# Moving the loads of a streaming attention decode from SyncE's queue to GpSimd's, with a one-packet flag

## The chip, the core and the metric

The kernel runs on one core of a Trainium2 chip. The metric is the device time of one execution in microseconds (us). Before the change it is 1918.17 us in the median of three runs (1917.4 to 1920.89).

## The reference

One token attends to a cache of 32 heads, 32,768 keys and values each, 192 wide, in bf16; a small dense block follows. Cut to what matters:

```python
q = (layernorm(x) @ wq).reshape(1, 1, 32, 192)              # 640 -> 6144
scores = einsum("bhqd,bhkd->bhqk", q, k_cache) * 192 ** -0.5
o = einsum("bhqk,bhkd->bhqd", softmax(scores), v_cache)
h = x + o.reshape(1, 1, 6144) @ wo
out = h + relu(layernorm(h) @ w1) @ w2
```

Both caches together are 805 MB, read once. Every other input is small beside them.

## The kernel before

A head's keys come in two loads of 6 MB into kt0 and kt1. Its values come in two loads of 3 MB into vb, one after the other, and one of 6 MB into va. In each, a partition receives one contiguous row of 48 KB or 24 KB. SyncE issues every load, when the buffer's last readers are done:

```python
def dma_program(g):                      # runs on SyncE
    def load(dst, src, sem, *label):
        g.do(lambda: nc.sync.dma_start(out=dst, in_=src), sem, label, by=16)
    ...
    for c in range(DT):                  # 5 loads of wq
        load(wq_c[c], ..., f"dwq{c}", "wq", c)
    for h in range(LAST):
        keys(h, 0); vals(h, 0); keys(h, 1)
        for ld in ((2, 1) if h == 0 else (1, 2)):
            vals(h, ld)                  # vals(h, 1) first waits for ("PV", h, 1)
        if h % 2 == 0:
            ...                          # wo of two heads
```

The loads of head 0 are thus keys 0, values 0 (vb), keys 1, values 2 (va), values 1 (vb again). GpSimd waits for each landing and passes it on with a semaphore increment, which TensorE (PE) and VectorE (DVE) wait for. PE takes a head's chunks in a fixed order; the first values are needed at its third chunk. ScalarE (ACT) copies and exponentiates.

The softmax here doesn't subtract the row's maximum and nothing guards it: scores larger than these inputs give would overflow.

## Time and profile before

| | before |
|---|---|
| time, median | 1918.17 us |
| span of the profiled run | 1915.3 us |
| busiest compute engine | DVE, 82% |
| DMA engines | full in all slices but the last, 431 GB/s |
| queue | one, SyncE's, 29,616 packet records |

The prediction below shows and reads the lines. In short: the stream of rows sets the pace of this kernel until the last keys land (at 1864.51 us; the DMA share is 1.00 from 120 to 1850 us); some 50 us of compute follow.

### The profile page before, as it was taken

What the parts mean: (1) busy time and instruction counts of PE and PEld (TensorE: products, weight loads), DVE (VectorE), ACT (ScalarE), POOL (GpSimd) and SP (SyncE); (2) the same over time, 40 slices, a digit from 0 to 9 for tenths busy, and PEclk for the clock granted to TensorE, in tenths of its full rate; (3) what the DMA queues carried; (4) which work ended last, traced back from release to release, by engine and by line L of the source; (5) the groups of instructions that cost most, each with busy time, mean ns of one, the idle gap of its engine ahead of it and who ended that gap; (6) DMA issues with size and microseconds to landing.
All of it is one profiled execution on the core that took longest, in us unless ns stands there. A gap on an engine that the chain in (4) does not pass through costs nothing.

```text
span 1915.3 us, 36109 instructions
## 1 busy us (share of the span) xinstructions
PE 1551.1 (81%) x15899; PEld 1085.0 (57%) x15899; DVE 1561.3 (82%) x731; ACT 939.5 (49%) x2000; POOL 1.0 (0%) x6
## 2 busy tenths in 40 slices
PE   7778887887878788877878877778788787877888
PEld 7555555655555555555556555556555555555555
DVE  2797787987878978789787888878798787987897
ACT  2455454554544544545545445445355454554444
POOL 0000000000000000000000000000000000000000
PEclk9888998888988889888898888898888898888988
DMA  9999999999999999999999999999999999999998
GB/s 409 430 434 433 430 435 431 435 436 433 434 431 434 435 429 431 435 432 439 434 429 435 434 431 435 434 429 437 431 434 438 431 436 429 437 431 433 431 432 367
DMA packets 29650, 825.29 MB, mean 431 GB/s; under 512 B 3131, under 2 KB 4668, under 8 KB 8124
## 3 DMA queue, kind: packets, MB, share of 16 engines
q1 hardware_dynamic: 29616, 824.98, 99.9%
q8 instruction: 15, 0.25, 0.0%
q14 instruction: 7, 0.06, 0.0%
q10 hardware_dynamic: 12, 0.00, 0.0%
HBM read 824.97 MB, written 0.00 MB: 431 GB/s over the span
## 4 chain that ended last, share of the span: by engine, by line
DVE 39%; DMA 38%; PE 15%; ACT 6%; issue 1%; DVEq 0%; POOLq 0%; SPq 0%
DMA kt<-in_A_k_cache_dram 36%; DVE sc L706 19%; DVE pr L703 18%; PE o_ps L360 7%; PE tp L379 6%; ACT kT L606 5%; DMA va<-in_A_v_cache_dram 2%; PE sp L360 1%; DVE o_pair L718 1%; ACT pA L621 1%; DVE oT L728 0%; DMA kt<-in_A_wq_dram 0%; DVE rec L711 0%; DVE rec L712 0%; DVE odd L724 0%
## 5 line engine op out<-in xcount | busy, mean ns | idle before, releaser
L703 DVE TENSOR_TENSOR pr<-kt,qb 128x2304 f32<-128x2304 bf16 (+2 forms) x257 | 756.7, 2944 | 314.8 <-POOLq L321 286.7
L606 ACT COPY kT<-tp 128x1024 bf16<-128x1024 bf16 (+1 forms) x898 | 814.3, 1017 | 272.9 <-PE tp L379 272.9
L379 PE MATMUL tp<-ident_f,kt 128*128 128x128 f32 x3456 | 588.4, 331 | 239.5 <-POOLq L342 162.9
L706 DVE TENSOR_REDUCE sc<-pr 128x12 f32<-128x2304 f32 (+2 forms) x257 | 756.1, 2942 | 8.9
L379 PEld LDWEIGHTS tp<-ident_f,kt 128*128 128x128 f32 x3456 | 482.7, 170 | 291.2 <-POOLq L342 168.7
L360 PE MATMUL o_ps<-va,pB 128*2 128x384 bf16 x1152 | 222.1, 341 | 65.0 <-POOLq L342 65.0
L360 PEld LDWEIGHTS sp<-qm,kT 128*128 128x128 bf16 x6912 | 197.2, 98 | 83.9 <-issue 42.8
L360 PE MATMUL sp<-qm,kT 128*128 128x2 bf16 x6912 | 214.5, 164 | 25.9 <-ACT pB L612 24.4
L360 PE MATMUL o_ps<-vb,pB 128*2 128x384 bf16 x1152 | 213.1, 331 | 22.9 <-ACT pA L621 22.3
L621 ACT ACTIVATE pA<-sc 128x12 bf16<-128x12 f32 (+2 forms) x257 | 58.2, 226 | 346.1 <-DVEq L65 346.1
L612 ACT ACTIVATE pB<-sp 128x20 bf16<-128x20 f32 (+2 forms) x258 | 52.4, 203 | 310.3 <-PE sp L360 310.3
L360 PEld LDWEIGHTS o_ps<-va,pB 128*2 128x2 bf16 x1152 | 94.4, 86 | 161.5 <-POOLq L342 72.4
L360 PE MATMUL o_ps<-va,pA 128*2 128x384 bf16 x896 | 172.2, 334 | 0.0
L360 PE MATMUL o_ps<-vb,pA 128*2 128x384 bf16 x896 | 166.7, 326 | 0.0
L360 PEld LDWEIGHTS o_ps<-vb,pB 128*2 128x2 bf16 x1152 | 89.9, 84 | 122.2 <-ACT pA L621 28.2
L360 PEld LDWEIGHTS o_ps<-va,pA 128*2 128x2 bf16 x896 | 77.4, 86 | 76.1 <-issue 9.6
L360 PEld LDWEIGHTS o_ps<-vb,pA 128*2 128x2 bf16 x896 | 75.2, 84 | 70.2
L612 ACT ACTIVATION_READ_ACCUMULATOR pB<-sp 128x1 f32 x258 | 55.1, 214 | 0.0
L621 ACT ACTIVATION_READ_ACCUMULATOR pA<-sc 128x1 f32 x257 | 53.1, 206 | 0.0
L360 PE MATMUL o_ps<-xn_ln,kt 128*96 128x1 bf16 (+1 forms) x316 | 22.3, 208 | 2.7 <-DMA kt<-in_A_wq_dram 2.7
L360 PEld LDWEIGHTS o_ps<-xn_ln,kt 128*96 128x96 bf16 (+1 forms) x316 | 22.1, 174 | 2.8 <-issue 2.7
L718 DVE TENSOR_SCALAR o_pair<-o_ps,rec 2x384 bf16<-2x384 f32 x32 | 19.4, 605 | 1.5 <-PE o_ps L360 0.4
(69 smaller groups left out, 186.5 us busy)
## 6 DMA issues: line engine op xcount, KB each, us to landing
kt<-in_A_k_cache_dram SPq DMA_DIRECT2D x62, 6144.0 KB, 26.8
vb<-in_A_v_cache_dram SPq DMA_DIRECT2D x63, 3072.0 KB, 20.8
va<-in_A_v_cache_dram SPq DMA_DIRECT2D x31, 6144.0 KB, 26.8
kt<-in_A_k_cache_dram SPq DMA_DIRECT2D x3, 3072.0 KB, 21.3
wo_s<-in_A_wo_dram SPq DMA_DIRECT2D x16, 480.0 KB, 19.0
kt<-in_A_wq_dram SPq DMA_DIRECT2D x4, 1536.0 KB, 10.9
va<-in_A_v_cache_dram SPq DMA_DIRECT2D x1, 3072.0 KB, 30.7
va<-in_A_v_cache_dram SPq DMA_DIRECT2D x2, 1536.0 KB, 35.5
```

Source lines behind the costliest of these rows:

```text
L360: return lambda: pe.matmul(o, lhsT=w, rhs=r, **kw)
L379: calls.append(lambda b=b, o=o: pe.transpose(out=dst[:, b, :], in_=src[:, o:o + 2 * P].bitcast(f32), identity=ident_f[:]))
L606: g.do(lambda: act.copy(out=kT[c % 2][:, b0:b0 + nb, :], in_=src[:, 0:nb, :].bitcast(bf16)), "act_pe", ("cp", h, c, k))
L612: g.do(lambda: act.activation(out=pB[c % NB][:, 0:jp], in_=sp[:, 0:jp], func=F.Exp, scale=SCALE, accum_out=dsums[:, 2 * c + 1:2 * c + 2]), ...
L621: g.do(lambda: act.activation(out=pA[c % NB][:, 0:jd], in_=sc[c % NC][:, 0:jd], func=F.Exp, scale=SCALE, accum_out=dsums[:, 2 * c:2 * c + ...
L703: g.chain(lambda: dve.tensor_tensor(out=pr[:, 0:j1 - j0, :], in0=src[:, (off + j0) * Dh:(off + j1) * Dh].rearrange("p (j d) -> p j d", d=D ...
L706: g.chain(lambda: dve.reduce_sum(out=sc[c % NC][:, j0:j1], in_=pr[:, 0:j1 - j0, :], axis=X), "dve")
L718: g.do(lambda: dve.tensor_scalar_mul(out=o_pair[:, :, 1, :], in0=o_ps[0:2, 0:2 * Dh].rearrange("q (i d) -> q i d", i=2), scalar1=rec[0:2, ...
```

## The change

Its intent is to take the cost of a packet out of the stream. The call that issues a load from GpSimd is given a flag, `single_packet`, that I took to ask for one packet for each load and DMA engine. Seven first loads stay on SyncE, because nothing has to be waited for there; SyncE passes on the landings in GpSimd's place. The place in the order of loads where the issuing goes over from SyncE to GpSimd is called the seam below.

```diff
-    def dma_program(g):
+    def first_loads(g):
         def load(dst, src, sem, *label):
             g.do(lambda: nc.sync.dma_start(out=dst, in_=src), sem, label, by=16)
+        for c in range(DT):
+            load(wq_c[c], ..., f"dwq{c}", "wq", c)
+        load(kt[0][:], rows(k_hd, 0, 0, JK), "dk_first", "k", 0, 0)
+        load(vb[:], rows(v_hd, 0, 0, JK)[:, 0:JL * Dh], "dv_first", "v", 0, 0)
+
+    def dma_program(g):
+        e = nc.gpsimd
+        ... (the two set-up instructions that GpSimd had before)
+        def load(dst, src, sem, *label):
+            g.do(lambda: e.dma_start(out=dst, in_=src, single_packet=True), sem, label, by=16)
...
-        g.do(lambda: nc.gpsimd.sem_inc(sems["pool_pe"], 1))
+        g.do(lambda: nc.sync.sem_inc(sems["pool_pe"], 1))
...
         @block.sync
-            dma_program(Program(book, sems, nc.sync))
+            relay_program(Program(book, sems, nc.sync))
         @block.gpsimd
-            pool_program(Program(book, sems, nc.gpsimd))
+            dma_program(Program(book, sems, nc.gpsimd))
```

More of the change, by code (lines that the diff above doesn't have):

```diff
@@ L221 @@
     names = ["pool_pe", "act_pe", "dve_pe", "act_dve", "dve_act", "dve", "dve_row", "pe_dve", "pool_row", "pool_dve", "pool_act", "pe_act", "pe", "dve_sp", "act_row"]
-    names += [f"dk{i}" for i in range(NK)] + ["dva", "dvb"] + ["dwo", "dx", "dout"] + [f"dwq{i}" for i in range(5)]
+    names += [f"dk{i}" for i in range(NK)] + ["dva", "dvb", "dk_first", "dv_first"] + ["dwo", "dx", "dout"] + [f"dwq{i}" for i in range(5)]
     names += [f"dke{i}" for i in range(4)] + ["dvh0", "dvh1"] + [f"dve{i}" for i in range(4)] + ["dw1"] + [f"dw2_{i}" for i in range(4)]
@@ L227, with rows @@
              "dve": ("pool_dve", "act_dve", "pe_dve", "dve")}
-    def dma_program(g):
+    def rows(src, h, k0, jl):
+        return src[h, k0:k0 + P * jl, :].rearrange("(p j) d -> p (j d)", p=P)
+    def first_loads(g):
         def load(dst, src, sem, *label):
             g.do(lambda: nc.sync.dma_start(out=dst, in_=src), sem, label, by=16)
-        def rows(src, h, k0, jl):
-            return src[h, k0:k0 + P * jl, :].rearrange("(p j) d -> p (j d)", p=P)
+        for c in range(DT):
+            load(wq_c[c], wq_view[:, c * H * Dh:(c + 1) * H * Dh], f"dwq{c}", "wq", c)
+        load(kt[0][:], rows(k_hd, 0, 0, JK), "dk_first", "k", 0, 0)
+        load(vb[:], rows(v_hd, 0, 0, JK)[:, 0:JL * Dh], "dv_first", "v", 0, 0)
+    def dma_program(g):
+        e = nc.gpsimd
+        g.do(lambda: e.memset(wide[:], 0.0), "pool_act", ("ident0",))
+        g.wait("ident0")
+        g.do(lambda: e.affine_select(out=wide[:], in_=wide[:], compare_op=A.not_equal, fill=1.0, base=HE,
+                                     pattern=[[-1, HE + P + 2 * (P - HE)]], channel_multiplier=1), "pool_row", ("ident",))
+        def load(dst, src, sem, *label):
+            g.do(lambda: e.dma_start(out=dst, in_=src, single_packet=True), sem, label, by=16)
         def keys(h, ld):
@@ L257, in vals @@
             load((vb, vb, va)[ld][:], src, "dva" if ld == 2 else "dvb", "v", h, ld)
-        for c in range(DT):
-            load(wq_c[c], wq_view[:, c * H * Dh:(c + 1) * H * Dh], f"dwq{c}", "wq", c)
         for h in range(LAST):
-            keys(h, 0)
-            vals(h, 0)
+            if h > 0:
+                keys(h, 0)
+                vals(h, 0)
             keys(h, 1)
@@ L310, in dma_program, with relay_program @@
             load(w2_s[:, c0:c1], B_w2.rearrange("(c p) n -> p c n", p=P)[:, c0:c1], f"dw2_{i}", "w2", i)
-    def pool_program(g):
-        e = nc.gpsimd
-        g.do(lambda: e.memset(wide[:], 0.0), "pool_act", ("ident0",))
-        g.wait("ident0")
-        g.do(lambda: e.affine_select(out=wide[:], in_=wide[:], compare_op=A.not_equal, fill=1.0, base=HE,
-                                     pattern=[[-1, HE + P + 2 * (P - HE)]], channel_multiplier=1), "pool_row", ("ident",))
+    def relay_program(g):
+        first_loads(g)
         def key(h, ld):
             relay(g, "k", h, ld)
-            g.do(lambda: nc.gpsimd.sem_inc(sems["pool_dve"], 1))
+            g.do(lambda: nc.sync.sem_inc(sems["pool_dve"], 1))
             book_relay(g, "k", h, ld, sem="pool_dve")
@@ L797 @@
     plan = Program(book, sems)
-    for f in (dma_program, pool_program):
+    for f in (relay_program, dma_program):
         f(plan)
```

## The prediction

> **What bounds the kernel now.** I read the page first: busy shares, then the DMA row of the slices and the packet count.
>
> ```profile
> PE 1551.1 (81%) x15899; PEld 1085.0 (57%) x15899; DVE 1561.3 (82%) x731; ACT 939.5 (49%) x2000; POOL 1.0 (0%) x6
> ...
> DMA  9999999999999999999999999999999999999998
> ...
> DMA packets 29650, 825.29 MB, mean 431 GB/s; under 512 B 3131, under 2 KB 4668, under 8 KB 8124
> ...
> q1 hardware_dynamic: 29616, 824.98, 99.9%
> ```
>
> No compute engine is above 82%, while the DMA row is full in every slice but the last, and one queue (q1, SyncE's) keeps the 16 DMA engines occupied for 99.9% of the span. The kernel streams both caches once; its time is the transfer plus a start and a tail. The table of stretches says where the rest is (columns: length, busy time of the engines, clock, DMA share, GB/s).
>
> ```profile
> 120.00:1850.00 1730.00, 1402.17 (x14250) 975.43 (x14249) 1438.17 (x647) 861.19 (x1832) 0.00 (x0) 0.88 1.00 433
> 1850.00:1916.00 66.00, 56.61 (x645) 37.13 (x642) 51.42 (x38) 31.42 (x72) 0.00 (x0) 0.90 0.91 382
> ```
>
> In the long middle the DMA share is 1.00 at 433 GB/s. The chain that ended last shows the tail: the last head's keys, then compute alone.
>
> ```profile
> 1836.82 27.69 DMA kt<-in_A_k_cache_dram
> 1864.56 0.04 issue
> 1864.61 1.86 PE tp L379 x15
> ```
>
> So up to about 1864 us a microsecond taken from the stream is a microsecond of the span, and each microsecond in which the queue is empty is lost; the last 50 us are PE and ACT work that this change does not touch.
>
> The packet records of the same trace (start, length, bytes of each) give the grain. The median packet of 49,152 B takes 1815 ns, of 24,576 B 912, of 12,288 B 460, of 3,840 B 149, of 1,280 B 55, and a 4 B semaphore write 9. A straight line through them is bytes / 27.2 B per ns plus 8 ns. Per engine q1 has 29,616 / 16 = 1,851 packets: 825 MB / 16 / 27.2 gives 1,896 us of bytes, 1,851 x 8 ns gives 15 us of packet cost, and the sum is the 1,912.5 us that the records add up to. This 15 us is the only thing in the stream that the change can take.
>
> [...] The trace shows a constant cost per packet too, but of 8 ns; on 48 KB rows it is 0.44%, small but paid 1,851 times. [...] Here SyncE issued at 0.96 us and the first data packet began at 1.97 us; GpSimd's is not in this trace.
>
> **The change, part by part.**
>
> *Packets, minus.* Seven loads stay with SyncE (five of wq, the first keys, the first values): 5 x 9 + 9 + 9 = 63 packets per engine with their semaphore writes. The other 188 loads carry 1,851 - 63 = 1,788. With one packet for each load and engine, 188 are left if the semaphore write rides in the same packet, 376 if not: 1,412 to 1,600 packets fewer, times 8 ns, 11.3 to 12.8 us. About 130 of them (vectors and weights of the tail) lie behind the last keys, where compute is the limit, so 1 us is not earned. **Gain 11 us**, if the cost belongs to the packet and not to the descriptor: no run shows that yet, I give it 70%.
>
> *Issue latency, little.* What the queue still has to do when a load is issued is its slack. I replayed all issues with the packet lengths above, each load behind the one before. Past the first head the smallest slack is 2.6 us for a load into vb and 3.2 for one into kt; medians are 7.0 and 9.7. [...] If it took over 2.5 us, perhaps a third of the 31 heads would lose a fraction each. **Plus 0 to 3, I take 0.5.**
>
> *Relay, nothing.* The pass-on of a landing moves from GpSimd to SyncE: 17 ns in the trace, the same wait and increment on another sequencer. GpSimd had 1.0 us of work in all. DVE, PE and ACT keep their order of instructions.
>
> *Start, the risk.* Here are two queues at once. The change keeps GpSimd's first load (second half of head 0's keys) behind the end of the queries, as before:
>
> ```profile
> 33.03 0.33 SPq L232 DMA_DIRECT2D kt<-in_A_k_cache_dram  x1
> 33.40 0.43 SPq L232 DMA_DIRECT2D va<-in_A_v_cache_dram  x1
> 37.65 5.54 PEld L379 LDWEIGHTS tp<-ident_f,kt 128*128 128x128 f32 x27 [3.83 <-POOLq L342]
> 47.03 1.78 PE L360 MATMUL o_ps<-vb,pB 128*2 128x384 bf16 x10 [1.18 <-ACT pA L621]
> 54.57 0.33 SPq L232 DMA_DIRECT2D vb<-in_A_v_cache_dram  x1
> ```
>
> At 33 us SyncE's queue still holds the last rows of the first keys (passed on at 37.6) and all eight rows per engine of the first values (their packets end at 44.6). In one queue the new loads stand behind them. [...] The bytes are the same, but the first values then land after both, at 37 + 29 + 7 = 73 us instead of 45[...]. The tensor engine needs the values at its third chunk; the release of vb, seen at 54.57, is about 10 us behind them. So vb would be asked for at 82 to 84 us with nothing queued since 73: 10 to 13 us of empty queue, plus some 3.5 before the next head's first keys. **Plus 13 to 17 us if whole packets alternate; 0 if the engines mix finer or the old queue wins.**
>
> *Tail, little.* w1 and w2 are 40 + 96 rows per engine[...]. I take 0.
>
> **The sum.** Good case: 1918.2 - 11 + 0.5 = 1907.5. Alternating case: 1907.5 + 15 = 1922. The arithmetic leaves me between two lumps. [...]that keeping seven loads on SyncE looks like the work of someone who watched the start favours the first. I choose near the middle, a little to the good side: **1911 us**.
>
> **The rivals.**
> (a) *Alternating packets starve the start*: as above, 1918 to 1926. [...] Against it: only the first two loads can overtake anything; after 75 us there is one data queue.
> (b) *The 8 ns belong to the descriptor*: then nothing is gained and the time is 1918 to 1921 without, up to 1935 with the start's loss. For it: the 4 B semaphore write costs the same 8 ns although it follows its rows directly.
> (c) *GpSimd is slow at writing descriptors*, and its issue takes the place of the queue as the bound[...]. A microsecond over it in every head costs 31 us: 1938. Against it: most loads have 7 us and more. I give it 6%.
> (d) *Instruction fetches wait behind long packets*: the trace has them as 16 KB packets on a queue of their own, one each 11 to 18 us in the first 153 us and again from 1867 on. [...]
>
> **Range and chances.** The good case, up to 5 us better if semaphore writes ride along and start or tail gain: 1902 and up. The bad one with (d) ends at 1928. The range 1902 to 1928 holds both lumps. Faster by 2% would be 1880 us, under the 1,896 us that the bytes alone take, so it is all but excluded (1%); over 1956 needs (c) in full (3%).
>
> **What would show it.** Packet cost: the count of packets falls from 29,650 to some 4,000 or 7,000, if the records are of packets, or the rows' own records shorten from 1815 to 1807 ns; the middle stretch rises from 433 to 435 GB/s at the same 1.00 share. If it stays at 433, the gain is refuted. Start: the first pass-on of keys later than 37.6 us, the first use of vb later than 47, and a DMA share under 1.00 between 70 and 100 us refute the good case. Issue latency: a share under 1.00 in the middle. Tail: the stretch from the last keys' landing to the end should stay at 50 us.

The sum came to 1918.2 - 11 + 0.5 = 1907.5 us in the good case and to 1907.5 + 15 = 1922 in the other, and 1911 was chosen between them. The 0.5 was a guess. The 15 are an estimate on a condition that no trace showed, "if whole packets alternate": the 29 us in it are two loads of eight rows of 1815 ns for an engine, the 7 the eight rows of 912 ns of the first values. Rival (d)'s term, an estimate of up to 5 us on top of the other case, is in the 1928. In rival (c), "over it" is over the slack of 2.6 us. The 435 GB/s are 16 times the fitted 27.2 B per ns.

## The result

The changed kernel takes 1920.24 us in the median of four runs (1919.19 to 1922.07), beside 1919.53 of the kernel before (four runs, 1917.4 to 1921.38). The ratio is 1.0005, with a 95% interval of 0.9991 to 1.0020. The predicted gain of 7 us isn't there; the time is the same.

The profile page of the changed kernel:

```profile
PE 1551.9 (81%) x15899; PEld 1083.6 (56%) x15899; DVE 1561.4 (81%) x731; ACT 938.8 (49%) x2000; POOL 101.5 (5%) x194
...
DMA packets 27026, 825.29 MB, mean 430 GB/s; under 512 B 3131, under 2 KB 3132, under 8 KB 5500
...
q0 software_dynamic: 25984, 807.68, 97.5%
q1 hardware_dynamic: 1008, 17.30, 2.1%
```

GpSimd (POOL) is now busy for 101.5 us and not for 1.0, nearly all of it in the instructions that issue its loads, about 0.53 us each, beside everything else. The bytes moved to its queue, q0. But the packets number 27,026, not the 4,000 to 7,000 of the prediction. By stretches (columns as in the prediction), first the start of the kernel before, then the changed kernel:

```profile
40.00:80.00 40.00, 29.42 (x312) 21.64 (x311) 38.63 (x15) 25.22 (x50) 0.00 (x0) 0.87 1.00 429
80.00:120.00 40.00, 33.05 (x348) 21.25 (x347) 28.28 (x16) 18.25 (x41) 0.00 (x0) 0.98 1.00 427
```

```profile
40.00:80.00 40.00, 24.82 (x266) 16.59 (x265) 38.63 (x15) 22.67 (x43) 1.06 (x2) 0.79 0.98 417
80.00:120.00 40.00, 35.09 (x389) 22.49 (x387) 24.95 (x15) 20.59 (x48) 2.63 (x5) 0.99 0.98 411
120.00:1850.00 1730.00, 1403.14 (x14250) 976.10 (x14251) 1440.87 (x648) 859.98 (x1828) 86.12 (x163) 0.88 1.00 433
```

The middle runs at 433 GB/s and a share of 1.00, to the digit as before. That refutes the gain by the prediction's own test. What was lost lies before 120 us, where the DMA share is 0.98 for 80 us and was 1.00. The packet records show more. The median record, read from the traces:

```
bytes    before, SyncE's queue     changed, GpSimd's queue
49,152   1815 ns  x11904           1815 ns  x11776
24,576    912 ns  x8576             912 ns  x8448
 7,680    291 ns  x256              291 ns  x1280   (mostly two 3,840 B rows joined)
 3,840    149 ns  x2048             none
```

A long row is a record of its own, of the same length as before. Short rows alone are joined. From the same records one can read when a share of all bytes has arrived. Such marks compare streams better than spans do, and I use them below:

| | 4% | 6% | 30% | 90% | 98% |
|---|---|---|---|---|---|
| before, us | 79.75 | 118.65 | 576.56 | 1718.77 | 1870.59 |
| changed, us | 80.92 | 121.78 | 579.64 | 1721.36 | 1873.40 |
| behind, us | 1.2 | 3.1 | 3.1 | 2.6 | 2.8 |

So 3.1 us are lost by 120 us, and half a microsecond comes back in the middle. How far such marks scatter shows the run without the flag, further below: its records turn out to be the same, and its marks lie 0.7 to 1.2 us before the changed kernel's, with 2.4 us lost at 6%. Differences of a microsecond between two marks are not read here. The timeline of the start shows what happened (start, length, engine, line, operation, tiles; in brackets the idle time before and what ended it):

```profile
33.25 0.68 POOL L250 DMA_DIRECT2D kt<-in_A_k_cache_dram  x1 [31.30 <-PE attT L371]
...
37.63 4.71 PE L390 MATMUL tp<-ident_f,kt 128*128 128x128 f32 x27 [3.79 <-SPq L353]
...
59.35 3.36 PE L371 MATMUL o_ps<-vb,pB 128*2 128x384 bf16 x10 [13.67 <-SPq L353]
...
69.65 0.53 POOL L250 DMA_DIRECT2D vb<-in_A_v_cache_dram  x1 [35.19 <-PE o_ps L371]
...
81.73 0.53 POOL L250 DMA_DIRECT2D kt<-in_A_k_cache_dram  x1 [11.02 <-PE o_ps L371]
```

The first keys are used at 37.63 as before, so nothing overtook them. The first values are used at 59.35 and not at 47.03: PE stood 13.67 us for them; the same line before had 1.18. The next load of vb was issued at 69.65 instead of 54.57, the next head's keys at 81.73 instead of 78.37. The engines had run, or were running, out of rows by then: by the records they miss 0.4 us in all around 72 us and 1.3 around 82, and the first rows after a gap take up to 3159 ns in place of 1815.

The chain that ended last shows a second, smaller loss in the changed kernel's tail:

```profile
1841.38 25.39 DMA kt<-in_A_k_cache_dram
...
1866.85 3.42 PE tp L390 x15
```

The same 15 transposes took 1.86 us before. Now PE had waited 1.81 us for these keys, and the table of stretches gives the granted clock (the last three columns are clock, DMA share and GB/s), first for before, then for the changed kernel:

```profile
1864.00:1868.00 4.00, 3.86 (x49) 2.96 (x46) 3.82 (x3) 3.26 (x7) 0.00 (x0) 1.00 0.97 416
```

```profile
1867.00:1870.50 3.50, 3.50 (x22) 3.19 (x23) 3.44 (x2) 2.78 (x5) 0.00 (x0) 0.56 1.00 426
```

After the wait PE runs at a clock of 0.56 where it had 1.00. The traces of later runs show the same at these 15 transposes. Two of them, without the flag and with nine loads from SyncE:

```profile
1865.64 3.28 PE L390 MATMUL tp<-ident_f,kt 128*128 128x128 f32 x15 [1.81 <-SPq L353]
```

```profile
1872.59 3.33 PE L394 MATMUL tp<-ident_f,kt 128*128 128x128 f32 x15 [1.79 <-SPq L357]
```

In four traces PE waits 1.79 to 2.05 us here, a drop of the clock begins within half a microsecond of the first transpose and lasts 3.4 us, and the transposes take 3.28 to 3.44 us (this kernel, these two runs, and 8 KB pieces without the flag). In five it waits under 0.4 us, the clock over them is full, and they take 1.84 to 1.86 (before, 8 KB pieces with the flag and from SyncE, the run that waits for the landing, eleven loads from SyncE). So the drop goes with the wait at this place. That the wait causes it is not shown, and it is no rule: elsewhere in the trace of before only 15 of 66 idle times of 1.8 us or more have a drop begin within half a microsecond of their end.

The last keys land 2.3 us later than before (1866.77, not 1864.51), the transposes end 3.8 us later, the span 4.1 us. So of the 4.1 us between the two profiled spans 2.3 come with the stream and 1.8 arise in the tail. They are one execution each, the one of before among the fastest of its four and that of the changed kernel among the slower; the timed runs bound the difference at -1.7 to 3.8 us, and with 0 in that interval no loss of time is shown.

### The profile page after: what moved, and what is told of

Same layout as the page of the kernel before. It is cut to its first block, busy times and chain, and to the rows that moved or that the text cites. A ratio compares the mean times of both kernels' runs of the same rounds, so it can differ in the third digit from the quotient of the medians.

```text
span 1919.4 us, 36109 instructions
## 1 busy us (share of the span) xinstructions
PE 1551.9 (81%) x15899; PEld 1083.6 (56%) x15899; DVE 1561.4 (81%) x731; ACT 938.8 (49%) x2000; POOL 101.5 (5%) x194
## 2 busy tenths in 40 slices
DMA packets 27026, 825.29 MB, mean 430 GB/s; under 512 B 3131, under 2 KB 3132, under 8 KB 5500
## 4 chain that ended last, share of the span: by engine, by line
DVE 39%; DMA 37%; PE 14%; ACT 6%; issue 2%; another core or an unknown queue 1%; DVEq 0%; SPq 0%; POOL 0%
DMA kt<-in_A_k_cache_dram 37%; DVE sc L717 19%; DVE pr L714 18%; PE o_ps L371 6%; PE tp L390 6%; ACT kT L617 6%; PE sp L371 1%; DVE o_pair L729 1%; ACT pA L632 1%; DVE oT L739 0%; DVE rec L722 0%; DVE rec L723 0%; DVE odd L735 0%; DVE o_pair L741 0%
## 5 line engine op out<-in xcount | busy, mean ns | idle before, releaser
L250 POOL DMA_DIRECT2D kt<-in_A_k_cache_dram x67 | 35.6, 531 | 840.5 <-PE o_ps L371 809.2
L250 POOL DMA_DIRECT2D vb<-in_A_v_cache_dram x66 | 34.9, 529 | 806.0 <-PE o_ps L371 806.0
L623 ACT ACTIVATION_READ_ACCUMULATOR pB<-sp 128x1 f32 x258 | 55.4, 215 | 0.0
## 6 DMA issues: line engine op xcount, KB each, us to landing
vb<-in_A_v_cache_dram SPq DMA_DIRECT2D x1, 3072.0 KB, 55.4
```

The source lines that it names most:

```text
L250: g.do(lambda: e.dma_start(out=dst, in_=src, single_packet=True), sem, label, by=16)
L623: g.do(lambda: act.activation(out=pB[c % NB][:, 0:jp], in_=sp[:, 0:jp], func=F.Exp, scale=SCALE, accum_out=dsums[:, 2 * c + 1:2 * c + 2]), ...
```

## The experiments

My theory after the result: the flag changes nothing, a long row is the unit of both cost and alternation, and what the changed kernel loses it loses where two queues are in flight. The rivals: the flag works, but cost or alternation lie elsewhere; GpSimd's later start of a load is the loss; GpSimd's queue is slower or faster by itself. Marks are from one profiled execution of each; times have three rounds, or five where said.

### No flag

```diff
-    e.dma_start(out=dst, in_=src, single_packet=True)
+    e.dma_start(out=dst, in_=src)
```

> The changed kernel with the one-packet flag taken away and nothing else. Theory: the 8 ns belong to each row that an engine moves, and the flag changes nothing that can be measured here. Then the time is the changed kernel's, ratio to before 1.000 to 1.003, a 49,152 B row still takes 1815 ns, the record count stays at 27,026 (the short wo rows still joined in pairs of 7,680 B), and the first values still land near 57 to 59 us. Rival: the flag does frame a load as one packet, and part of the cost or of the start's alternation comes from it. Then rows get longer than 1815 ns or short rows are no longer joined (29,650 records), or the first values land at another time than 59 us.

Measured: 1919.34 us beside 1917.73, ratio 1.0005 (0.9989 to 1.0022). The page of this run:

```profile
DMA packets 27026, 825.29 MB, mean 430 GB/s; under 512 B 3131, under 2 KB 3132, under 8 KB 5500
```

Every record size and count is the changed kernel's, and the median lengths too: 1815 ns for the long rows, the short ones joined as with the flag. The first values land 55.2 us after their issue, with the flag 55.4. The flag did nothing that shows. GpSimd's queue joins the short rows here without it, too (27,026 records, not 29,650). Why the flag is without effect, no run tells.

### Pieces of 8 KB: what costs, and what an engine finishes before it switches

```diff
-    e.dma_start(out=dst, in_=src, single_packet=True)
+    e.dma_start(out=dst, in_=src, single_packet=True, max_dma_last_dim=8192)   # with the flag
+    e.dma_start(out=dst, in_=src, max_dma_last_dim=8192)                       # without
```

> The changed kernel with every row of GpSimd's loads cut into pieces of at most 8,192 B (six for a 48 KB row), flag kept: up to 49 pieces for a load and engine. Theory (cost for each piece, whatever the flag): 4,760 more pieces per engine at 8 ns are 38 us, ratio to before 1.018 to 1.022, and a piece takes 309 ns. Rival (cost for each packet, which the flag makes one for a load and engine): no longer than the changed kernel, ratio 0.998 to 1.004. At the start the order of pieces in the two queues shows what an engine finishes before it switches: one piece of 8 KB for one row of SyncE's (first values then land near 48 us) or six (59 us) or a whole load (59 us and later).

> As the run before it, with the flag taken away. Theory: the flag is without effect, so everything is as with it: ratio to before 1.018 to 1.022, piece 309 ns, same record count and the same order at the start. Rival (the flag makes one packet): this run is 38 us longer than the run with the flag, and engines switch between the queues more often at the start.

Measured: with the flag 1941.87 us, ratio 1.0117 (1.0100 to 1.0134); without it 1941.94, ratio 1.0121 (1.0104 to 1.0138). With the flag, and then without:

```profile
DMA packets 103186, 825.29 MB, mean 425 GB/s; under 512 B 3131, under 2 KB 3132, under 8 KB 6268
```

```profile
DMA packets 103186, 825.29 MB, mean 425 GB/s; under 512 B 3131, under 2 KB 3132, under 8 KB 6268
```

The two are alike again. Pieces do cost, so the rival of a free ride in one packet falls. But the size was missed: 22 us beside the changed kernel's 1920.24, and not the 38 of the theory. The records add up to more than the time in which they lie: a piece's record is 309 ns, of which some 3 overlap the next (an estimate: the 8 ns by the lengths less the 4.8 below). The marks give the true cost: from 30% to 90% of the bytes the stream takes 1155.9 us in both, against 1142.2 before; 13.7 us over 0.6 x 4,760 pieces is **4.8 ns** for each. (Counting the records between the marks, against the changed kernel or before, gives 4.7 to 4.8.)

The order at the start shows the alternation. The records carry no engine number; I strung them into 16 chains, each record behind one that ends where it begins. One chain from 31 us on (s is SyncE's queue, G GpSimd's, with KB; the last rows of the first keys are s48, the first values s24):

```
changed kernel   s48 s48 s48 s24 s24 G48 s24 G48 s24 G48 s24 G48 s24 G48 s24 G48 s24 G48 G48 G48
8 KB pieces      s48 s48 s48 s24 s24 s24 G8 s24 G8 s24 G8 s24 G8 s24 G8 s24 G8 G8 G8 G8 ...
```

In these chains an engine takes one row, or piece, from each queue in turn. With 8 KB pieces little can overtake a row of SyncE's, and the first values land 43.3 us after their issue in place of 55.4. With a 48 KB row between any two of them they are 12 us later. Alternation is real, but by rows, with the flag set.

These two runs also test what the loss at the start comes from, better than the runs that I made for it: issuer and seam are the changed kernel's, and only the rows of GpSimd's queue are shorter. The values are used at 47.22 and 47.42 us, and the 6% marks are at 120.6 and 120.9. The kernel before with the same pieces, next below, is at 120.2. So some 0.5 us are lost to it, or 1 if that kernel's 96 further pieces are set off (at 4.7 ns, an estimate), where whole rows lost 2.4 to 3.1. Most of the loss goes when the rows between the values get short; the rest is near the scatter of the marks.

### Pieces of 8 KB from SyncE

```diff
-    nc.sync.dma_start(out=dst, in_=src)          # the kernel before
+    nc.sync.dma_start(out=dst, in_=src, max_dma_last_dim=8192)
```

> The kernel before, SyncE issuing everything, with every row cut into pieces of at most 8,192 B: 4,856 more pieces per engine. Theory: a piece costs the same whoever issues it. From the two runs with GpSimd's pieces, whose bytes from 30% to 90% took 1155.9 us against 1142.2 in the kernel before, a piece costs 4.8 ns (the records overlap by some 3 ns, so their 8 ns are too much): 23 us, ratio to before 1.010 to 1.014. Rival: GpSimd's queue already joins the cost of several pieces and SyncE's does not. Then this one pays the 8 ns of its records, 39 us, ratio 1.018 to 1.022.

Measured: 1940.10 us beside 1919.23, ratio 1.0112 (1.0097 to 1.0127), and 1156.0 us from 30% to 90%. That is 13.8 us over 0.6 x 4,856 pieces, 4.7 ns each. The theory holds: a piece of 8 KB costs the same from either queue.

### Pieces of 2 KB from each queue

```diff
+    max_dma_last_dim=2048   for the two-dimensional loads: caches and wq
```

It was added to the changed kernel without the flag, and to the kernel before.

> The changed kernel without the flag, with every row of the caches' loads cut into pieces of at most 2,048 B (24 for a 48 KB row). GpSimd's queue was seen to join short rows into records of up to 8 KB (two of 3,840 B, two of 3,072 B, four of 1,280 B), flag or not. Theory: it joins four pieces of 2,048 B into one of 8,192 B, which costs what such a piece costs alone: records of 8,192 B at 309 ns as in the runs with 8 KB pieces, ratio to before 1.010 to 1.016. Rival: the cost stays with the piece and the joining is only in the records: about 23,300 more pieces per engine at 4.8 ns are 112 us, ratio 1.05 to 1.07.

> The kernel before, SyncE issuing everything, with the same cut to 2,048 B. Theory: SyncE's queue doesn't join, so every piece pays: records of 2,048 B, 112 us more, ratio to before 1.05 to 1.07. Rival (a piece costs the same 4.8 ns at most down to where something hides it, or SyncE's queue joins too): ratio below 1.03.

Measured: from GpSimd 1983.96 us, ratio 1.0335 (1.0318 to 1.0352); from SyncE 2027.21, ratio 1.0563 (1.0545 to 1.0580). First GpSimd's, then SyncE's page:

```profile
DMA packets 199827, 825.29 MB, mean 416 GB/s; under 512 B 3132, under 2 KB 3181, under 8 KB 198909
```

```profile
DMA packets 404690, 825.29 MB, mean 408 GB/s; under 512 B 3131, under 2 KB 7228, under 8 KB 404668
```

SyncE's run is as expected: no joining, and 66.6 us more from 30% to 90% for 0.6 x 23,440 records, again 4.7 ns. For GpSimd both expectations missed. Pieces are joined, but in pairs of 4,096 B and not in fours. The joined sizes of all runs, but for 80 smaller records, are 2 x 2,048, 2 x 3,072, 2 x 3,840, 3 x 1,536, 3 x 1,920 and 4 x 1,280 B. So joining stopped at 4,096 B or more, and 3,840 B (2 x 1,920 or 3 x 1,280) still took one more row. And joining does pay: 40.0 us more from 30% to 90% where SyncE has 66.6. But it doesn't make the second row free: over the 6,700 further records between the marks, 40 us are 6.0 ns for a joined pair, beside 4.7 for one 2 KB record and 9.4 for two. Some 1.3 ns stay with the second row. Rows of 6,144 B and more had a record each in the changed kernel, and its cache rows are mostly of 24 and 48 KB.

### Loads of 64 partitions, flag kept

```diff
-    g.do(lambda: e.dma_start(out=dst, in_=src, single_packet=True), sem, label, by=16)
+    g.do(lambda: e.dma_start(out=dst[0:P // 2], in_=src[0:P // 2], single_packet=True), sem, None, by=16)
+    g.do(lambda: e.dma_start(out=dst[P // 2:P], in_=src[P // 2:P], single_packet=True), sem, label, by=16)
```

> The changed kernel with each of GpSimd's loads issued as two of 64 partitions, flag kept. [...] Theory: the flag stays without effect: a 49,152 B row still takes 1815 ns, 188 more semaphore writes at 9 ns are 1.7 us per engine, and two issues in place of one delay some loads: ratio to before 1.000 to 1.006. Rival: the flag takes effect at 64 rows: rows in one packet lose their own cost, the 30% to 90% stretch falls from 1142.2 towards 1138 us, and the ratio is below 0.999.

(No run shows a limit for the rows of a packet.)

Measured: 3892.5 us, ratio 2.014 (2.004 to 2.025). Both expectations missed, and the run says nothing of the cost of a row, because something else took over (the stretch from 120 to 3850 us):

```profile
120.00:3850.00 3730.00, 1608.36 (x15012) 1084.25 (x15009) 1509.10 (x684) 907.52 (x1933) 182.22 (x358) 0.70 1.00 210
```

The DMA share is full at 210 GB/s in place of 433, and a 49,152 B record takes 3804 ns in place of 1815. Why the stream runs at half its rate in loads of 64 partitions, no run tests. One thing can be read all the same: at the start these flagged loads alternate with the first values by rows, too (one or two at a time). So it isn't for its 128 rows that a load's flag is without effect.

### Moving the seam: nine loads from SyncE

```diff
         load(vb[:], ..., "dv_first", "v", 0, 0)
+        g.wait("att0")                             # the end of the queries, as for GpSimd
+        load(kt[1][:], rows(k_hd, 0, P * JK, JK), "dk1_first", "k", 0, 1)
+        load(va[:], rows(v_hd, 0, P * JK, JK), "dva_first", "v", 0, 2)
```

GpSimd leaves these two out and begins with the second load of vb.

> The changed kernel, but SyncE issues nine loads first instead of seven, so that no load of GpSimd's is in flight beside one of SyncE's. Theory: the 3.1 us that the changed kernel has lost when 6% of the bytes are in (121.8 us against 118.7) come from the two queues alternating at the start. Then the first values land at 45 us again, the 6% mark is at 118.7 within 0.5, and the time is 2.5 to 3.5 us below the changed kernel's: ratio to before 0.998 to 1.000. Rival: the loss comes from GpSimd's later start of each load, which finds the queue empty. Then the mark stays at 121 or later and the ratio at 1.000 to 1.003.

Measured: 1925.64 us beside 1917.73, ratio 1.0035 (1.0018 to 1.0051): slower by 0.35%, clear of noise though small. The theory missed; the rival's mark (121 or later) is met, but not its ratio. The 6% mark is at 127.3. The timeline:

```profile
54.65 0.68 POOL L253 DMA_DIRECT2D vb<-in_A_v_cache_dram  x1 [52.70 <-PE o_ps L375]
...
81.45 3.36 PE L375 MATMUL o_ps<-va,pB 128*2 128x384 bf16 x10 [12.56 <-SPq L357]
...
87.03 0.53 POOL L253 DMA_DIRECT2D kt<-in_A_k_cache_dram  x1 [31.16 <-PE o_ps L375]
```

The load of vb is issued at 54.65, as in the kernel before, so the first seam is gone. But now SyncE's va load is still on its way, and GpSimd's rows of vb go in between. va is used at 81.45 instead of 74.08, the next head's keys are issued at 87.03 instead of 78.37, and by the records the engines miss 7.5 us in all from 80 to 88 us. I had looked only at the seam that I removed. I read this as the theory's mechanism at another place: a load somebody waits for shares the engines with one that is needed later. The timeline shows it for this execution; that nothing else adds to the 8.7 us isn't shown.

### No overlap by waiting

```diff
             elif ld == 1:
                 g.wait("att0")
+                g.wait("v", 0, 0)                  # the first values have landed
```

> The changed kernel, but GpSimd's first load waits until the first values have landed, so the queues don't overlap there, and the engines are idle from the last row of SyncE's until GpSimd's first row. Theory: the first values are used at 47 us as before; an idle gap of 2 to 4 us (landing, wait, descriptors, first row), so the 6% mark is 120.5 to 122.5 and the time 2 to 4 us above before's: the same loss as the changed kernel's, by another way. Rival (the loss is not from the overlap): the changed kernel's loss comes on top, 6% mark at 124 or later.

Measured: 1923.98 us beside 1919.23, ratio 1.0028 (1.0013 to 1.0044), 6% mark at 125.1. This is above the theory's 122.5, and by its letter (124 or later) the rival's outcome. The values are used at 46.87 us, as before. The timeline and the stretch from 40 to 50 us:

```profile
45.45 0.68 POOL L250 DMA_DIRECT2D kt<-in_A_k_cache_dram  x1 [43.50 <-DMA vb<-in_A_v_cache_dram]
```

```profile
40.00:50.00 10.00, 8.67 (x96) 6.87 (x95) 9.64 (x5) 9.97 (x15) 1.22 (x2) 1.00 0.70 265
```

The gap that the wait makes is 4 us of engine time between 40 and 48 us, the upper end of what I had expected, and another 0.7 around 84 us follows from it. The first row begins 1.39 us after GpSimd starts on the load; from SyncE it was 1.01 us in the kernel before, one case of each. And the engines' first rows after the gap take 2585 ns in the mean in place of 1815. Gap, slow rows and the second gap make 5.5 of the 6.5 us by which the mark is late. I had taken the gap too small; about 1 us is left, so a part of the rival is not excluded.

### Moving the seam to where nobody waits: eleven loads from SyncE

```diff
         load(va[:], rows(v_hd, 0, P * JK, JK), "dva_first", "v", 0, 2)
...
+        g.wait("PV", 0, 1)                         # after passing on the first keys and values
+        load(vb[:], rows(v_hd, 0, 0, JK)[:, JL * Dh:2 * JL * Dh], "dvb_first", "v", 0, 1)
+        load(wo_s[:], wo_view[0], "dwo_first", "wo", 0)
```

It comes on top of the nine; GpSimd begins with head 1.

> The changed kernel with SyncE issuing the first eleven loads, all of head 0. GpSimd begins with the next head's first keys at 78 us, when SyncE's queue holds hardly more than the output weights, which nobody waits for. Theory (the loss of the changed kernel, and the larger one of the run with nine loads first, are rows of the old queue held up by rows of the new one where somebody waits for them): the 6% mark comes back to 118.7 within 0.7 us and the time to the kernel before's, ratio 0.998 to 1.001. Rival (GpSimd's later start of a load costs a little at every load that finds a short queue): the 6% mark is back but the 90% mark is 2 us or more behind before's 1718.8, and the ratio is 1.001 or more.

Measured, five rounds: 1919.45 us beside 1919.23, ratio 1.0005 (0.9991 to 1.0019). The 6% mark is at 119.9, 1.2 us behind before's and not 3.1 or 8.7. So removing the overlap of waited-for rows removes more than half of the loss at the start (3.1 in the changed kernel, 2.4 without the flag), which the theory said, though it promised 0.7; the difference is within the scatter of the marks. The 90% mark is 2.9 us behind, as the rival said: between 50% and 70% this execution loses 1.1 us, in part where the engines miss 0.4 us near 1292 us, after a load that GpSimd issued late. The changed kernel shows no such gap there. With one execution of each I can't say how often it occurs. The time can't be told from before's, nor from the changed kernel's: its ratio is 1.0005 as well.

No version beats the kernel before. By an estimate from these figures there was little to win: if a long row costs the 4.8 ns of a piece, all 1,851 records of an engine cost 9 us, and nothing found takes that from long rows.

## Why the prediction was wrong

**The step that failed** is "Packets, minus": the gain of 11 us, "if the cost belongs to the packet and not to the descriptor", which I gave 70%. What failed is a condition ahead of that one. I took for granted that the flag would make one packet of a load. It made none: record sizes and counts are the same with and without it, for 48 KB rows, for 8 KB pieces and, by their alternation, for loads of 64 rows. The condition that I doubted holds in part where rows are joined at all: a pair of 2 KB rows in one record costs 6.0 ns in place of 9.4, so most of the cost goes with the record, but some 1.3 ns stay with each further row.

**The size was off too.** I read 8 ns from the lengths of records. Records overlap, and four pairs of runs put the cost at 4.7 to 4.8 ns. Had the flag saved the 1,412 to 1,600 packets less the 130 of the tail, the gain would have been 6 to 7 us and not 11, or about 5 if each joined row keeps 1.3 ns (estimates from these runs). A check was at hand and I passed over it: the records sum to 1,912.5 us, more than the 1,908.7 us from the start of the first to the end of the last, so they must overlap. Two sums are slightly off as well: 1918.2 - 11 + 0.5 is 1907.7, and 1,896 + 15 is 1,911, not 1,912.5.

**Rival (a)** was right in kind and wrong in grain. Two queues do take turns at the start. But they do so by rows, so the first values came at 59 us, not 73, and the keys weren't held up. "0 if the engines mix finer" was wrong as well: mixing row by row still cost 12 us of lateness for those values, and 2.4 to 3.1 us of the stream by the 6% mark. The 13 to 17 us for whole packets met no run that has them. The chain from late values to a late reuse of vb to an empty queue was as told.

**Rival (b)** names the outcome, "nothing is gained" with 1918 to 1921 us, and its reason only in part: each long row kept a record of its own, of 1815 ns, with the flag and without.

**Issue latency** as predicted: 1.39 us to the first row beside SyncE's 1.01, one case of each, a share of 1.00 in the middle, and no gap from 600 to 1700 us in the changed kernel's records; the run with eleven loads shows that one can occur. **Rival (c)** is refuted: 0.53 us a load. **The relay** cost nothing: 17 ns, as before. **Tail**: I took 0 and the profiled run shows 1.8 us. 1.6 of them lie in the 15 transposes, where PE had waited 1.81 us for the late keys and then had a clock of 0.56. **Rival (d)** isn't tested by the runs.

That the range held the time is luck: it was drawn around two lumps, and neither was the right one. The sum of the profiled run is 0 for the flag, +3.1 at the start, -0.8 from there to the last keys (not attributed; near the scatter of the marks) and +1.8 in the tail; the timed runs allow anything from -1.7 to 3.8.

## What to carry to other kernels

Before counting on a flag, run it with and without and look at the count and sizes of the packet records. Measure a cost for each row from the time that the bytes take with more and fewer rows, not from the lengths of records, which overlap (8 ns by the lengths here, 4.7 to 4.8 by the time). Here the row costs mattered in 2 KB pieces (5.6% of the time from SyncE's queue, 3.4% from GpSimd's, which joined them in pairs), and hardly in rows of 24 or 48 KB (9 us, 0.5%, by the estimate above). Where two queues feed the same engines, a load somebody waits for can be slowed by one that is needed later (here the first values were used at 59.35 us in place of 47.03): look for a place for the seam where nothing urgent is in flight, and check the next load behind a seam that you move. (The worst place tried cost 0.35%; that a good one gains time isn't shown.)
